# A fused adaLN, linear-attention and SwiGLU kernel: the load order of row tile 2 and the division of the first row tiles' normalisation and values

## The chip, the cores and the metric

The kernel runs on one core of one Trainium2 chip. The metric is the device time of one execution in microseconds (us); before the change its median over three runs is 828.99 us (828.73 to 829.15). Five engines work beside each other on the core, each in its own order: TensorE (PE in the profile; its weight loads are PEld), VectorE (DVE), ScalarE (ACT), GpSimd (POOL) and SyncE (SP), which here only issues transfers. Transfers (DMA) fetch from the chip's memory into on-chip tiles; matmuls write into PSUM tiles.

## The reference, cut to what matters

```python
def reference(A_x, A_wqkv, A_wo, B_x, B_w_gate, B_w_up, B_w_down, c, w_mod):
    # _A_ref: linear attention, 32 heads; q, k, v = h @ wqkv; phi(q) (sum phi(k) v) / (phi(q) sum phi(k)), @ wo
    # _B_ref: (silu(x @ w_gate) * (x @ w_up)) @ w_down
    x = A_x                                              # (1, 2048, 1024), bfloat16
    mod = (_silu(c) @ w_mod).reshape(c.shape[0], 6, 1, -1)
    sa, ca, ga, sb, cb, gb = (mod[:, 0].copy(), ..., mod[:, 5].copy())
    h = _layernorm(x, axis=-1) * (1 + ca) + sa
    x = x + ga * _A_ref(h, A_wqkv, A_wo)
    h = _layernorm(x, axis=-1) * (1 + cb) + sb
    x = x + gb * _B_ref(h, B_w_gate, B_w_up, B_w_down)
    return x
```

The change is in the opening alone: the layer norm of the first four row tiles (128 rows of 1024 each), their scale `1 + ca`, and the value projection `h @ wqkv[:, 2D:]` of those 512 rows. The shift `sa` has no part in these first values (it is put in later as one row), so they need only the normalised rows, turned, and times the scale.

## The kernel before: the opening

Loads are issued in program order on SyncE's queue. A block of weights is 128 x 1024 in bfloat16, 256 KB, and so is a row tile. The first half of the scale's weights is `wca[0]` (four pieces of 256 KB, the first from ScalarE's queue), the second half `wca[1]`; `wsa` are the shift's weights.

```python
    for st in range(3):
        load_x(st, nc.sync)
    nc.scalar.dma_start(out=c_sb[:], in_=c_v)
    # ... tiles ...
    load_ca(0, nc.scalar)
    nc.scalar.dma_start(out=sc_row[0:1, :], in_=c)
    for cc in range(4):
        load_block(wv, wqkv_v, cc, 2 * D)
    load_ca(1, nc.sync)
    load_x(3, nc.sync)
    for cc in range(4, DC):
        load_block(wv, wqkv_v, cc, 2 * D)
    for j in range(DC):
        load_block(wsa, wm_v, j, 0)
    for cc in range(DC):
        load_block(wk, wqkv_v, cc, D)
```

The statistics of a row tile are two `bn_stats` and a `bn_aggr` on VectorE, a small add there, and a power on GpSimd; `normalise_act` does a further small operation on GpSimd and then the tile on ScalarE. `bn` is a generator, so that its three steps can be laid between other VectorE work.

```python
    def rstd_of(mv, n):
        veps = small.tile([P, STC], F32, name="veps")
        last_veps[0] = nc.vector.tensor_scalar_add(out=veps[:, 0:n], in0=mv[:, 0:n, 1], scalar1=LN_EPS)
        rstd = small.tile([P, STC], F32, name="rstd")
        nc.gpsimd.tensor_tensor(out=rstd[:, 0:n], in0=veps[:, 0:n], in1=neg_half[:].to_broadcast([P, n]), op=ALU.pow)
        return rstd

    def bn(src, mv_out):
        stats = small.tile([P, NNB, nc.vector.BN_STATS_DIM], F32, name="stats")
        for i in range(NNB):
            nc.vector.bn_stats(out=stats[:, i, :], in_=src[:, i * NB:(i + 1) * NB])
            yield
        nc.vector.bn_aggr(out=mv_out, in_=stats[:])
        yield

    def normalise_act(dst, src, mv, rstd, pieces=1):
        nmr = small.tile([P, 1], F32, name="nmr")
        last_nmr[0] = nc.gpsimd.tensor_scalar(out=nmr[:], in0=mv[:, 0, 0:1], scalar1=rstd[:, 0:1], scalar2=-1.0,
                                op0=ALU.mult, op1=ALU.mult)
        w = src.shape[-1] // pieces
        for i in range(pieces):
            ws = slice(i * w, (i + 1) * w)
            nc.scalar.activation(out=dst[:, ws], in_=src[:, ws], func=ACT.Identity, bias=nmr[:], scale=rstd[:, 0:1])
```

The opening proper. `in_order` keeps VectorE, ScalarE and GpSimd in this order each; matmuls and transposes keep program order too. [...] `hs` holds the turned, scaled rows, `hT` the turned ones without scale. `v_mms(hs, gs, accs, lo, hi)` issues, for each column block `cc` from lo to hi, one 128 x 512 matmul for each group (row tile, half of the values) in `gs`.

```python
    H = 2 * P
    with in_order(nc.vector, nc.scalar, nc.gpsimd):
        mod_ps = acc_b("mod_ps")
        mm(mod_ps[:, 0:DC], lhsT=c_sb[:], rhs=ident[0:DC, 0:DC], start=True, stop=True)
        nc.scalar.activation(out=scT[:], in_=mod_ps[:, 0:DC], func=ACT.Silu)
        xn0 = ln1_norm(*ln1_stats(0, 0), 2)
        _, _, x1_sb, mv1, rstd1 = ln1_stats(0, 1)
        x2_sb = x_tiles.pop(2)
        mv2 = small.tile([P, STC, 2], F32, name="mv")
        bn2 = bn(x2_sb, mv2[:, 0, :])
        next(bn2)
        xn1 = k2.tile([P, D], BF16, name="xn", bufs=4)
        nc.vector.tensor_scalar(out=xn1[:, 0:NB], in0=x1_sb[:, 0:NB], scalar1=mv1[:, 0, 0:1], scalar2=rstd1[:, 0:1],
                                op0=ALU.subtract, op1=ALU.mult)
        normalise_act(xn1[:, NB:], x1_sb[:, NB:], mv1, rstd1)
        next(bn2)
        col0 = acc_b("col0")
        cols = [col0[:, 0:1]] + [mod_ps[:, DC + i:DC + i + 1] for i in range(3)]
        tps = [acc_b("tp", (4, H), BF16) for _ in range(2)]

        def turn_half(xn, t, h):
            for i in range(4):
                transpose(tps[h][:, i, t * P:(t + 1) * P], xn[:, (4 * h + i) * P:(4 * h + i + 1) * P])

        def ca_cols(k):
            for i in range(4):
                for j in (2 * k, 2 * k + 1):
                    mm(cols[i], lhsT=wca[0][:, j, i * P:(i + 1) * P], rhs=scT[:, j:j + 1], start=False,
                       stop=j == DC - 1 and i in (0, 3))

        mm(cols[0], lhsT=ident[:], rhs=base_t[:, 0:1], start=True, stop=False)
        keep_warm(P)
        mm(mod_ps[:, DC:DC + 3], lhsT=ident[:], rhs=base_t[:, 0:3], start=True, stop=False)
        keep_warm(2 * P)
        ca_cols(0)
        keep_warm(2 * P, P)
        ca_cols(1)
        turn_half(xn0, 0, 0)
        ca_cols(2)
        keep_warm(P)
        turn_half(xn0, 0, 1)
        turn_half(xn1, 1, 0)
        ca_cols(3)
        keep_warm(P)

        def scale_first(cc):
            nc.vector.tensor_scalar(out=hs[:, cc, 0:H], in0=tps[0][:, cc, :], scalar1=cols[cc], scalar2=None, op0=ALU.mult)

        scale_first(0)
        next(bn2)
        rstd2 = rstd_of(mv2, 1)
        for cc in range(1, 4):
            scale_first(cc)
        nc.scalar.copy(out=ca0T[:, 0:1], in_=cols[0])
        nc.scalar.copy(out=ca0T[:, 1:4], in_=mod_ps[:, DC:DC + 3])
        xn2 = ln1_norm(0, 2, x2_sb, mv2, rstd2)
        nc.scalar.copy(out=hT[:, 0:4, 0:H], in_=tps[0][:])
        nc.vector.tensor_copy(out=sc32[:], in_=scT[:].unsqueeze(2).to_broadcast([P, DC, DH]))
        gs = k_groups[0:4]
        v_mms(hs, gs, accs, 0, 1)
        turn_half(xn1, 1, 1)
        nc.scalar.copy(out=hT[:, 4:8, 0:H], in_=tps[1][:])
        nc.scalar.activation(out=sc_row[0:1, :], in_=sc_row[0:1, :], func=ACT.Silu)
        v_mms(hs, gs, accs, 1, 3)
        tp2 = turn_tile(xn2)
        for cc in range(4):
            scale_turned(tp2, cc, 2)
        nc.scalar.copy(out=hT[:, :, H:H + P], in_=tp2[:])
        v_mms(hs, gs, accs, 3, 4)
        ca_rows()
        mod_turn(DC + 4, 2 * DC)
        nc.vector.tensor_scalar_add(out=ca0T[:, 4:8], in0=ca0T[:, 4:8], scalar1=1.0)
        for cc in range(4, DC):
            scale_to(hs, hT, cc, 0, H)
        gs2, accs2 = k_groups[4:6], [acc_b("acc") for _ in range(2)]
        v_mms(hs, gs2, accs2, 0, 4)
        xn3 = ln1_norm(*ln1_stats(0, 3))
        for cc in range(4, DC):
            scale_to(hs, hT, cc, H, H + P)
        v_mms(hs, gs, accs, 4, DC)
        v_evac(0, gs, accs)
        v_mms(hs, gs2[0:1], accs2[0:1], 4, DC)
        tp3 = turn_tile(xn3)
        for cc in range(DC):
            scale_turned(tp3, cc, 3)
        nc.scalar.copy(out=hT[:, :, H + P:], in_=tp3[:])
        v_mms(hs, gs2[1:2], accs2[1:2], 4, DC)
        v_evac(0, gs2, accs2)
        gs3, accs3 = k_groups[6:8], [acc_a() for _ in range(2)]
        v_mms(hs, gs3[0:1], accs3[0:1])
        mod_rows(lambda j: wsa[j // 4][:, j % 4, :], 0, DC)
        mod_turn(0, DC)
        nc.vector.tensor_copy(out=sca[:], in_=scr[:, :, :, 0])
        v_mms(hs, gs3[1:2], accs3[1:2])
        v_evac(0, gs3, accs3)
        for lo in (0, H):
            for cc in range(DC):
                modulate(hT, cc, ca1T, saT, lo, lo + H)
        nc.vector.tensor_copy(out=sc32[:], in_=saT.unsqueeze(2).to_broadcast([P, DC, DH]))
```

Here `scale_first(cc)` is one VectorE operation `hs[:, cc, 0:256] = tps[0][:, cc, :] * cols[cc]`, which reads PSUM; `keep_warm` are matmuls whose result is overwritten; `ca_rows` are 32 narrow matmuls for the second half of the scale, `mod_rows` 32 for the shift and the rest; `mod_turn` turns their rows into columns on VectorE. After this part the keys (`k_mms`) follow, which read `hT` as `modulate` left it, and then the rest of the kernel, the same before and after.

Of the kernel before, what the change touches and what calls it, by code (L numbers as in the profile page):

```python
# [21 lines left out]
def kernel(  # L22
# [100 lines left out]
        last_load[0] = eng.dma_start(out=x_sb[:], in_=x2[st * P:(st + 1) * P, :])  # L123
        x_tiles[st] = x_sb

    for st in range(3):
        load_x(st, nc.sync)
    nc.scalar.dma_start(out=c_sb[:], in_=c_v)

# [5 lines left out]
    def load_block(tiles, view, cc, lo, eng=nc.sync):  # L135
        eng.dma_start(out=tiles[cc // 4][:, cc % 4, :], in_=view[:, cc, lo:lo + D])

    def load_ca(h, eng0):
        for k in range(4):
            js = slice(2 * k, 2 * k + 2)  # L140
            (eng0 if k == 0 else nc.sync).dma_start(out=wca[h][:, js, :], in_=wm_v[:, js, D + h * NB:D + (h + 1) * NB])
# [2 lines left out]
    nc.scalar.dma_start(out=sc_row[0:1, :], in_=c)  # L144
    for cc in range(4):
        load_block(wv, wqkv_v, cc, 2 * D)
    load_ca(1, nc.sync)
    load_x(3, nc.sync)
    for cc in range(4, DC):
# [55 lines left out]
    def bn(src, mv_out):  # L205
        stats = small.tile([P, NNB, nc.vector.BN_STATS_DIM], F32, name="stats")
        for i in range(NNB):
            nc.vector.bn_stats(out=stats[:, i, :], in_=src[:, i * NB:(i + 1) * NB])
            yield
        nc.vector.bn_aggr(out=mv_out, in_=stats[:])  # L210
        yield

    def normalise_act(dst, src, mv, rstd, pieces=1):
        nmr = small.tile([P, 1], F32, name="nmr")
# [11 lines left out]
    def turn_tile(xn):  # L226
# [2 lines left out]
            transpose(tp[:, cc, :], xn[:, cc * P:(cc + 1) * P])  # L229
        return tp  # L230

    hTs = {}

    def ln1_stats(sc, t):
        x_sb = x_tiles.pop(sc * STC + t)
        mv = small.tile([P, STC, 2], F32, name="mv")
        for _ in bn(x_sb, mv[:, 0, :]):
            pass
        rstd = rstd_of(mv, 1)
        return sc, t, x_sb, mv, rstd  # L240

# [224 lines left out]
    def keep_warm(*widths):  # L466
        for n in widths:
            mm(accs[3][:, 0:n], lhsT=neg_half[:].to_broadcast([P, P]), rhs=neg_half[:].to_broadcast([P, n]), start=True, stop=True)
# [8 lines left out]
# [3 lines that stand above are left out]
        nc.scalar.activation(out=scT[:], in_=mod_ps[:, 0:DC], func=ACT.Silu)  # L480
        xn0 = ln1_norm(*ln1_stats(0, 0), 2)
        _, _, x1_sb, mv1, rstd1 = ln1_stats(0, 1)
        x2_sb = x_tiles.pop(2)
        mv2 = small.tile([P, STC, 2], F32, name="mv")
        bn2 = bn(x2_sb, mv2[:, 0, :])
        next(bn2)
        xn1 = k2.tile([P, D], BF16, name="xn", bufs=4)
        nc.vector.tensor_scalar(out=xn1[:, 0:NB], in0=x1_sb[:, 0:NB], scalar1=mv1[:, 0, 0:1], scalar2=rstd1[:, 0:1],
                                op0=ALU.subtract, op1=ALU.mult)
        normalise_act(xn1[:, NB:], x1_sb[:, NB:], mv1, rstd1)  # L490
        next(bn2)
        col0 = acc_b("col0")
        cols = [col0[:, 0:1]] + [mod_ps[:, DC + i:DC + i + 1] for i in range(3)]
        tps = [acc_b("tp", (4, H), BF16) for _ in range(2)]
# [17 lines that stand above are left out]
        ca_cols(1)  # L512
        turn_half(xn0, 0, 0)
        ca_cols(2)
        keep_warm(P)
        turn_half(xn0, 0, 1)
        turn_half(xn1, 1, 0)
        ca_cols(3)
        keep_warm(P)

        def scale_first(cc):
            nc.vector.tensor_scalar(out=hs[:, cc, 0:H], in0=tps[0][:, cc, :], scalar1=cols[cc], scalar2=None, op0=ALU.mult)

        scale_first(0)
        next(bn2)
        rstd2 = rstd_of(mv2, 1)
        for cc in range(1, 4):
            scale_first(cc)
        nc.scalar.copy(out=ca0T[:, 0:1], in_=cols[0])
        nc.scalar.copy(out=ca0T[:, 1:4], in_=mod_ps[:, DC:DC + 3])  # L530
        xn2 = ln1_norm(0, 2, x2_sb, mv2, rstd2)
        nc.scalar.copy(out=hT[:, 0:4, 0:H], in_=tps[0][:])
        nc.vector.tensor_copy(out=sc32[:], in_=scT[:].unsqueeze(2).to_broadcast([P, DC, DH]))
        gs = k_groups[0:4]
        v_mms(hs, gs, accs, 0, 1)
        turn_half(xn1, 1, 1)
        nc.scalar.copy(out=hT[:, 4:8, 0:H], in_=tps[1][:])
        nc.scalar.activation(out=sc_row[0:1, :], in_=sc_row[0:1, :], func=ACT.Silu)
        v_mms(hs, gs, accs, 1, 3)
        tp2 = turn_tile(xn2)  # L540
        for cc in range(4):
            scale_turned(tp2, cc, 2)
        nc.scalar.copy(out=hT[:, :, H:H + P], in_=tp2[:])
        v_mms(hs, gs, accs, 3, 4)
        ca_rows()
        mod_turn(DC + 4, 2 * DC)
        nc.vector.tensor_scalar_add(out=ca0T[:, 4:8], in0=ca0T[:, 4:8], scalar1=1.0)
        for cc in range(4, DC):
            scale_to(hs, hT, cc, 0, H)
        gs2, accs2 = k_groups[4:6], [acc_b("acc") for _ in range(2)]  # L550
        v_mms(hs, gs2, accs2, 0, 4)
        xn3 = ln1_norm(*ln1_stats(0, 3))
        for cc in range(4, DC):
            scale_to(hs, hT, cc, H, H + P)
# [8 lines that stand above are left out]
        v_evac(0, gs2, accs2)  # L563
        gs3, accs3 = k_groups[6:8], [acc_a() for _ in range(2)]
        v_mms(hs, gs3[0:1], accs3[0:1])
        mod_rows(lambda j: wsa[j // 4][:, j % 4, :], 0, DC)
        mod_turn(0, DC)
        nc.vector.tensor_copy(out=sca[:], in_=scr[:, :, :, 0])
        v_mms(hs, gs3[1:2], accs3[1:2])
        v_evac(0, gs3, accs3)  # L570
        for lo in (0, H):
            for cc in range(DC):
                modulate(hT, cc, ca1T, saT, lo, lo + H)
        nc.vector.tensor_copy(out=sc32[:], in_=saT.unsqueeze(2).to_broadcast([P, DC, DH]))
    for st in range(STC, 2 * STC):
        load_x(st, nc.sync)
# [267 lines left out]
```

## Time and profile before

| what | value | where from |
|---|---|---|
| median time | 828.99 us (828.73 to 829.15) | three runs |
| span of the profiled execution | 827.1 us | the page's head |
| PE busy | 822.5 us (99%) | the page, part 1 |
| VectorE, ScalarE, GpSimd busy | 345.9, 173.6, 65.2 us | the page, part 1 |
| first value matmul | at 9.22 us | PE's timeline |
| first key matmul | at 26.14 us | PE's timeline |
| TensorE clock granted | full in all slices | the page, part 2 |

How to read it: PE is busy for nearly all of the span, so what the opening takes on PE before and between its matmuls is passed on to the end. Times in a timeline are start and length in us. An operation's listed length is longer than its share when operations of one engine follow each other closely; the distance from one start to the next is then what each costs. Matmul ends are modelled.

### The profile page before, as it was taken

The numbers are of one execution on the slowest core, as the hardware profiler recorded it, in microseconds if no ns is written. First come the engines' busy times: TensorE is split into PE (matmuls) and PEld (weight loads), VectorE is DVE, ScalarE is ACT, GpSimd is POOL, SyncE is SP. The second block draws the span as 40 slices with busy tenths as digits, with TensorE's granted clock in tenths as the row PEclk, the third lists the DMA queues.
The fourth block names the chain that finished last, engine by engine and source line by source line (L and its number), as shares of the span: only waits on it lengthen the run. The fifth ranks groups of instructions, "written<-read, shape, count | busy, mean of one in ns | idle before, by whom it ended". The sixth has DMA issues, their size and how long they took to land.

```text
span 827.1 us, 11346 instructions
## 1 busy us (share of the span) xinstructions
PE 822.5 (99%) x4629; PEld 379.8 (46%) x4629; DVE 345.9 (42%) x683; ACT 173.6 (21%) x261; POOL 65.2 (8%) x167
## 2 busy tenths in 40 slices
PE   9999999999999999999999999999999999999998
PEld 5444444444444444444444444444444444444444
DVE  5878778886353344421111353211114432222222
ACT  5545443434111101101111010111111101111000
POOL 3101110120313001000000010000001100000000
PEclk9999999999999999999999999999999999999999
DMA  9989544149995726456252272753405529710011
GB/s 342 307 180 205 115 107 100 44 117 318 374 230 184 262 100 190 142 170 214 82 171 84 66 223 86 253 185 113 142 1 183 147 67 342 235 44 1 18 59 52
DMA packets 143414, 129.33 MB, mean 156 GB/s; under 512 B 58817, under 2 KB 122817, under 8 KB 142850
## 3 DMA queue, kind: packets, MB, share of 16 engines
q1 hardware_dynamic: 139248, 115.36, 46.6%
q0 software_dynamic: 3824, 12.98, 5.1%
q8 instruction: 36, 0.59, 0.3%
q10 hardware_dynamic: 290, 0.27, 0.1%
q14 instruction: 16, 0.13, 0.1%
HBM read 102.24 MB, written 12.72 MB: 139 GB/s over the span
## 4 chain that ended last, share of the span: by engine, by line
PE 99%; DMA 1%; SPq 0%; DVE 0%; issue 0%
PE acc L98 91%; PE a_ps L98 7%; DMA wme<-in_w_mod_dram 1%; PE kvp L98 1%; PE mod_ps L98 0%; PE tp L101 0%; PE den L98 0%; SPq L123 0%; PE wf L98 0%; PE vb L98 0%; PE col L98 0%; DVE e L760 0%; DVE ob L763 0%
## 5 line engine op out<-in xcount | busy, mean ns | idle before, releaser
L98 PE MATMUL acc<-h2T,wgu 128*128 128x512 bf16 x1792 | 387.6, 379 | 0.0
L98 PEld LDWEIGHTS <-wgu 128*128 128x128 bf16 x1792 | 175.3, 98 | 211.3
L739 DVE TENSOR_TENSOR gu<-acc,e 128x512 bf16<-128x512 f32 x112 | 77.4, 691 | 289.9 <-PE acc L98 287.1
L98 PE MATMUL acc<-wd,gu 128*128 128x512 bf16 (+2 forms) x924 | 196.1, 373 | 0.0
L738 ACT ACTIVATE e<-acc 128x512 f32<-128x512 f32 x112 | 66.9, 597 | 374.8 <-PE acc L98 374.8
L98 PEld LDWEIGHTS <-gu 128*128 128x128 bf16 x924 | 89.3, 98 | 104.5
L760 DVE TENSOR_TENSOR e<-acc,gb_bc 128x512 f32<-128x512 f32 (+2 forms) x33 | 22.3, 675 | 131.6 <-PE acc L98 128.7
L98 PEld LDWEIGHTS <-hT 128*128 128x128 bf16 x448 | 43.6, 98 | 52.3
L98 PE MATMUL a_ps<-wof,pq 128*128 128x512 bf16 x256 | 57.4, 379 | 0.0
L98 PE MATMUL acc<-hT,wq 128*128 128x512 bf16 x256 | 56.6, 379 | 0.0
L98 PE MATMUL acc<-wk,hT 128*128 128x512 bf16 x256 | 56.4, 379 | 0.0
L284 ACT ACTIVATE eb<-acc 128x512 bf16<-128x512 f32 x64 | 37.5, 594 | 60.3 <-PE acc L98 56.6
L220 ACT ACTIVATE xn<-x,nmr,rstd 128x1024 bf16<-128x1024 f32 x16 | 19.8, 1241 | 126.2 <-POOL nmr L215 123.2
L98 PE MATMUL acc<-wv,hT 128*128 128x512 bf16 x192 | 41.9, 379 | 0.0
L707 POOL DMA_DIRECT2D x_scratch<-x x16 | 9.8, 615 | 373.5 <-DVE x L700 373.4
L98 PEld LDWEIGHTS <-pq 128*128 128x128 bf16 x256 | 25.1, 98 | 30.2
L98 PEld LDWEIGHTS <-wq 128*128 128x128 bf16 x256 | 24.7, 98 | 30.7 <-issue 1.7
L285 DVE TENSOR_SCALAR eb<-eb 128x512 bf16<-128x512 bf16 x64 | 18.2, 289 | 26.4 <-ACT eb L284 26.4
L700 DVE TENSOR_TENSOR x<-a_ps,x_sb 128x512 f32<-128x512 f32 x32 | 22.1, 691 | 8.6 <-PE a_ps L98 8.6
L202 POOL TENSOR_TENSOR rstd<-veps,neg_half 128x1 f32<-128x1 f32 x32 | 18.0, 562 | 91.8 <-DVE veps L200 70.1
L220 ACT ACTIVATE xn<-x_sb,nmr,rstd 128x1024 bf16<-128x1024 bf16 (+1 forms) x17 | 19.5, 1163 | 16.0 <-POOL nmr L215 15.9
L763 DVE TENSOR_TENSOR ob<-e,x1r 128x512 bf16<-128x512 f32 (+2 forms) x33 | 22.3, 675 | 1.0
(106 smaller groups left out, 330.0 us busy)
## 6 DMA issues: line engine op xcount, KB each, us to landing
wgu<-in_B_w_gate_dram SPq DMA_DIRECT2D x28, 1024.0 KB, 7.3
wgu<-in_B_w_up_dram SPq DMA_DIRECT2D x28, 1024.0 KB, 8.1
x_sb<-in_A_x_dram SPq DMA_DIRECT2D x32, 256.0 KB, 5.3
x_scratch<-x POOLq DMA_DIRECT2D x16, 512.0 KB, 3.3
x1r<-x_scratch SPq DMA_DIRECT2D x31, 256.0 KB, 2.9
wd<-in_B_w_down_dram SPq DMA_DIRECT2D x7, 1024.0 KB, 5.8
rbc<-rden_scratch POOLq DMA_DIRECT2D x16, 256.0 KB, 7.1
out_dram<-ob SPq DMA_DIRECT2D x31, 128.0 KB, 1.7
```

Of the source, the lines that this page charges most:

```text
L98: return tc.keep_in_program_order(nc.tensor.matmul(out, lhsT=lhsT, rhs=rhs, start=start, stop=stop))
L202: nc.gpsimd.tensor_tensor(out=rstd[:, 0:n], in0=veps[:, 0:n], in1=neg_half[:].to_broadcast([P, n]), op=ALU.pow)
L220: nc.scalar.activation(out=dst[:, ws], in_=src[:, ws], func=ACT.Identity, bias=nmr[:], scale=rstd[:, 0:1])
L284: nc.scalar.activation(out=e[:], in_=acc, func=ACT.Exp)
L285: nc.vector.tensor_scalar(out=e[:], in0=e[:], scalar1=1.0, scalar2=PHI_EPS, op0=ALU.min, op1=ALU.add)
L700: nc.vector.tensor_tensor(out=x1[:, ns], in0=a_ps[:], in1=x_t[:, ns], op=ALU.add)
L707: nc.gpsimd.dma_start(out=x1_dram[st * P:(st + 1) * P, :], in_=x1[:])
L738: nc.scalar.activation(out=sg[:], in_=ps[0][:], func=ACT.Silu)
L739: gm = nc.vector.tensor_tensor(out=guT[sc][f // GPT][:, f % GPT, :], in0=ps[1][:], in1=sg[:], op=ALU.mult)
L760: nc.vector.tensor_tensor(out=yt, in0=y_ps, in1=gb_bc[:, ns], op=ALU.mult)
L763: nc.vector.tensor_tensor(out=ob, in0=yt, in1=x1r, op=ALU.add)
```

## The change

It delays the load of row tile 2 until the first value-weight block is issued, so that the pieces of `wca[0]` and that block come one place earlier on the queue. Row tile 1 is normalised on VectorE in one operation instead of half there and half on ScalarE. Tile 2's statistics move behind the scaling of the first rows, and its normalisation is divided between VectorE and ScalarE. Both halves of tile 1 are turned before the first value matmul. Tile 2's transposes are divided into four before and four after the second scale rows (`ca_rows`), with the first value matmuls of tile 2 around those. Two `keep_warm` go. At the end of the part, the last values lie partly before `mod_rows`, and the eight `modulate` of `hT` take 512 columns each where sixteen took 256.

```diff
--- before.py
+++ after.py
@@ -123,7 +123,7 @@
         last_load[0] = eng.dma_start(out=x_sb[:], in_=x2[st * P:(st + 1) * P, :])
         x_tiles[st] = x_sb
 
-    for st in range(3):
+    for st in range(2):
         load_x(st, nc.sync)
     nc.scalar.dma_start(out=c_sb[:], in_=c_v)
 
@@ -144,6 +144,8 @@
     nc.scalar.dma_start(out=sc_row[0:1, :], in_=c)
     for cc in range(4):
         load_block(wv, wqkv_v, cc, 2 * D)
+        if cc == 0:
+            load_x(2, nc.sync)
     load_ca(1, nc.sync)
     load_x(3, nc.sync)
     for cc in range(4, DC):
@@ -206,9 +208,7 @@
         stats = small.tile([P, NNB, nc.vector.BN_STATS_DIM], F32, name="stats")
         for i in range(NNB):
             nc.vector.bn_stats(out=stats[:, i, :], in_=src[:, i * NB:(i + 1) * NB])
-            yield
         nc.vector.bn_aggr(out=mv_out, in_=stats[:])
-        yield
 
     def normalise_act(dst, src, mv, rstd, pieces=1):
         nmr = small.tile([P, 1], F32, name="nmr")
@@ -229,13 +229,19 @@
             transpose(tp[:, cc, :], xn[:, cc * P:(cc + 1) * P])
         return tp
 
+    def norm_split(src, mv, rstd):
+        xn = k2.tile([P, D], BF16, name="xn", bufs=4)
+        nc.vector.tensor_scalar(out=xn[:, 0:NB], in0=src[:, 0:NB], scalar1=mv[:, 0, 0:1], scalar2=rstd[:, 0:1],
+                                op0=ALU.subtract, op1=ALU.mult)
+        normalise_act(xn[:, NB:], src[:, NB:], mv, rstd)
+        return xn
+
     hTs = {}
 
     def ln1_stats(sc, t):
         x_sb = x_tiles.pop(sc * STC + t)
         mv = small.tile([P, STC, 2], F32, name="mv")
-        for _ in bn(x_sb, mv[:, 0, :]):
-            pass
+        bn(x_sb, mv[:, 0, :])
         rstd = rstd_of(mv, 1)
         return sc, t, x_sb, mv, rstd
 
@@ -480,15 +486,9 @@
         nc.scalar.activation(out=scT[:], in_=mod_ps[:, 0:DC], func=ACT.Silu)
         xn0 = ln1_norm(*ln1_stats(0, 0), 2)
         _, _, x1_sb, mv1, rstd1 = ln1_stats(0, 1)
-        x2_sb = x_tiles.pop(2)
-        mv2 = small.tile([P, STC, 2], F32, name="mv")
-        bn2 = bn(x2_sb, mv2[:, 0, :])
-        next(bn2)
         xn1 = k2.tile([P, D], BF16, name="xn", bufs=4)
-        nc.vector.tensor_scalar(out=xn1[:, 0:NB], in0=x1_sb[:, 0:NB], scalar1=mv1[:, 0, 0:1], scalar2=rstd1[:, 0:1],
+        nc.vector.tensor_scalar(out=xn1[:], in0=x1_sb[:], scalar1=mv1[:, 0, 0:1], scalar2=rstd1[:, 0:1],
                                 op0=ALU.subtract, op1=ALU.mult)
-        normalise_act(xn1[:, NB:], x1_sb[:, NB:], mv1, rstd1)
-        next(bn2)
         col0 = acc_b("col0")
         cols = [col0[:, 0:1]] + [mod_ps[:, DC + i:DC + i + 1] for i in range(3)]
         tps = [acc_b("tp", (4, H), BF16) for _ in range(2)]
@@ -512,43 +512,45 @@
         ca_cols(1)
         turn_half(xn0, 0, 0)
         ca_cols(2)
-        keep_warm(P)
         turn_half(xn0, 0, 1)
+        ca_cols(3)
         turn_half(xn1, 1, 0)
-        ca_cols(3)
-        keep_warm(P)
-
-        def scale_first(cc):
-            nc.vector.tensor_scalar(out=hs[:, cc, 0:H], in0=tps[0][:, cc, :], scalar1=cols[cc], scalar2=None, op0=ALU.mult)
-
-        scale_first(0)
-        next(bn2)
-        rstd2 = rstd_of(mv2, 1)
+        turn_half(xn1, 1, 1)
+
+        def scale_first(cc, lo, hi):
+            nc.vector.tensor_scalar(out=hs[:, cc, lo:hi], in0=tps[0][:, cc, lo:hi], scalar1=cols[cc], scalar2=None, op0=ALU.mult)
+
+        scale_first(0, 0, P)
+        scale_first(0, P, H)
         for cc in range(1, 4):
-            scale_first(cc)
+            scale_first(cc, 0, H)
         nc.scalar.copy(out=ca0T[:, 0:1], in_=cols[0])
         nc.scalar.copy(out=ca0T[:, 1:4], in_=mod_ps[:, DC:DC + 3])
-        xn2 = ln1_norm(0, 2, x2_sb, mv2, rstd2)
         nc.scalar.copy(out=hT[:, 0:4, 0:H], in_=tps[0][:])
-        nc.vector.tensor_copy(out=sc32[:], in_=scT[:].unsqueeze(2).to_broadcast([P, DC, DH]))
         gs = k_groups[0:4]
         v_mms(hs, gs, accs, 0, 1)
-        turn_half(xn1, 1, 1)
         nc.scalar.copy(out=hT[:, 4:8, 0:H], in_=tps[1][:])
-        nc.scalar.activation(out=sc_row[0:1, :], in_=sc_row[0:1, :], func=ACT.Silu)
-        v_mms(hs, gs, accs, 1, 3)
-        tp2 = turn_tile(xn2)
+        _, _, x2_sb, mv2, rstd2 = ln1_stats(0, 2)
+        nc.vector.tensor_copy(out=sc32[:], in_=scT[:].unsqueeze(2).to_broadcast([P, DC, DH]))
+        xn2 = norm_split(x2_sb, mv2, rstd2)
+        v_mms(hs, gs, accs, 1, 4)
+        tp2 = acc_b("tp", (DC, P), BF16)
+        for cc in range(4):
+            transpose(tp2[:, cc, :], xn2[:, cc * P:(cc + 1) * P])
         for cc in range(4):
             scale_turned(tp2, cc, 2)
-        nc.scalar.copy(out=hT[:, :, H:H + P], in_=tp2[:])
-        v_mms(hs, gs, accs, 3, 4)
+        gs2, accs2 = k_groups[4:6], [acc_b("acc") for _ in range(2)]
+        v_mms(hs, gs2, accs2, 0, 2)
         ca_rows()
         mod_turn(DC + 4, 2 * DC)
         nc.vector.tensor_scalar_add(out=ca0T[:, 4:8], in0=ca0T[:, 4:8], scalar1=1.0)
         for cc in range(4, DC):
             scale_to(hs, hT, cc, 0, H)
-        gs2, accs2 = k_groups[4:6], [acc_b("acc") for _ in range(2)]
-        v_mms(hs, gs2, accs2, 0, 4)
+        for cc in range(4, DC):
+            transpose(tp2[:, cc, :], xn2[:, cc * P:(cc + 1) * P])
+        nc.scalar.copy(out=hT[:, :, H:H + P], in_=tp2[:])
+        nc.scalar.activation(out=sc_row[0:1, :], in_=sc_row[0:1, :], func=ACT.Silu)
+        v_mms(hs, gs2, accs2, 2, 4)
         xn3 = ln1_norm(*ln1_stats(0, 3))
         for cc in range(4, DC):
             scale_to(hs, hT, cc, H, H + P)
@@ -563,14 +565,13 @@
         v_evac(0, gs2, accs2)
         gs3, accs3 = k_groups[6:8], [acc_a() for _ in range(2)]
         v_mms(hs, gs3[0:1], accs3[0:1])
+        v_mms(hs, gs3[1:2], accs3[1:2], 0, 2)
         mod_rows(lambda j: wsa[j // 4][:, j % 4, :], 0, DC)
         mod_turn(0, DC)
         nc.vector.tensor_copy(out=sca[:], in_=scr[:, :, :, 0])
-        v_mms(hs, gs3[1:2], accs3[1:2])
+        v_mms(hs, gs3[1:2], accs3[1:2], 2, DC)
         v_evac(0, gs3, accs3)
-        for lo in (0, H):
-            for cc in range(DC):
-                modulate(hT, cc, ca1T, saT, lo, lo + H)
+        modulate_all(hT, ca1T, saT)
         nc.vector.tensor_copy(out=sc32[:], in_=saT.unsqueeze(2).to_broadcast([P, DC, DH]))
     for st in range(STC, 2 * STC):
         load_x(st, nc.sync)
```

## The prediction

> **What bounds the kernel now.** The page's chain of the work that ended last comes first: PE takes 99% of it, so only what TensorE does, or waits for, can move the end. The waits of PE come next, over the whole span:
>
> ```profile
> PE 99%; DMA 1%; SPq 0%; DVE 0%; issue 0%
> PE acc L98 <- DVE neg_half L159: 0.9, 1, 0.9
> PE col L98 <- DMA wme<-in_w_mod_dram: 0.6, 1, 0.6
> ```
>
> PE waits 1.5 us in all, and all of it lies before the first value matmul. Behind that point nothing later can swallow a shift: a microsecond lost or won in the opening is a microsecond at the end. So I read PE's timeline of the opening (start, length, operation, count):
>
> ```profile
> 7.27 0.40 PE L101 MATMUL tp<-ident,xn 128*128 128x128 bf16 x4
> 9.22 1.04 PE L98 MATMUL acc<-wv,hs 128*128 128x512 bf16 x4
> 10.10 0.39 PE L101 MATMUL tp<-ident,xn 128*128 128x128 bf16 x4
> 10.32 1.89 PE L98 MATMUL acc<-wv,hs 128*128 128x512 bf16 x8
> 12.05 0.61 PE L101 MATMUL tp<-ident,xn 128*128 128x128 bf16 x8
> 12.49 1.03 PE L98 MATMUL acc<-wv,hs 128*128 128x512 bf16 x4
> 13.45 0.84 PE L98 MATMUL mod_ps<-wme,sc 128*32 128x128 bf16 x32
> 14.23 6.22 PE L98 MATMUL acc<-wv,hs 128*128 128x512 bf16 x28
> ```
>
> From 9.22 to the first key matmul at 26.14 there is no hole: 28 matmuls from 14.23 to 20.28 are 0.216 us each, eight transposes from 12.05 to 12.49 are 0.055 each, `ca_rows` from 13.45 to 14.23 is 0.78. What feeds this is VectorE's timeline:
>
> ```profile
> 6.89 0.68 DVE L208 BATCH_NORM_STATS2 stats<-x_sb 128x6 f32<-128x512 bf16 x1
> 7.65 0.41 DVE L488 TENSOR_SCALAR xn<-x_sb,mv,rstd 128x512 bf16<-128x512 bf16 x1
> 7.97 0.69 DVE L208 BATCH_NORM_STATS2 stats<-x_sb 128x6 f32<-128x512 bf16 x1
> 8.81 0.35 DVE L522 TENSOR_SCALAR hs<-tp,col 128x256 bf16<-128x256 bf16 x1 [0.15 <-PE col L98]
> 9.08 0.20 DVE L210 BATCH_NORM_AGGREGATE mv<-stats 128x2 f32<-128x12 f32 x1
> 9.40 0.88 DVE L522 TENSOR_SCALAR hs<-tp,mod_ps 128x256 bf16<-128x256 bf16 x3
> 12.77 0.86 DVE L277 TENSOR_SCALAR hs<-tp,e 128x128 bf16<-128x128 bf16 x4 [2.29 <-PE tp L101]
> ```
>
> Two things are to be seen. Tile 2's statistics (6.89 and 7.97) sit in holes in which VectorE waits for GpSimd or PE, so they cost nothing. And the scaling of tile 2 at 12.77 waits for all eight transposes (modelled end 12.05 + 0.61 = 12.66), though its first operation reads only one; meanwhile PE has matmuls and `ca_rows` up to 14.23.
>
> [...] `modulate` takes 0.34 us for 256 columns and 0.41 for 512, so 0.07 per 256 more, and the PSUM reads 0.274 for 128 and 0.35 for 256, so 0.07 per 128. [...] the record gives the full clock throughout, with a hole of 0.6 us.
>
> **Part 1, the load.** `wca[0]`'s last three pieces and the first `wv` block move up by 256 KB. From 5 to 10 us the queues move 383 GB/s, so 0.262 MB / 383 GB/s = 0.7 us earlier. This removes the wait of 0.6 at 6.33 to 6.94, but the next thing on PE is the transposing of tile 0, which starts at 7.27 because ScalarE's first half of it, from 6.40, takes 0.8. Tiles 0 and 1 land first in either version, and VectorE goes from 3.63 to 6.97 with hardly a hole. So the earlier weights alone win nothing: they end in a longer wait for tile 0. Tile 2 becomes the eighth block, 2.1 MB: 1.0 MB by 5 us (203 GB/s x 5), the other 1.1 at 383 GB/s, so at 7.9, plus about 1 us until it is seen (that offset is from the fifth block: 1.31 MB have passed at 5.8 by the same sum, and PE was let go at 6.9). At 8.9 it is in time for what follows.
>
> **Part 2, the first value matmul.** The power for tile 1 still ends at 7.61, so VectorE's whole-tile normalisation starts at 7.65. Its 1024 columns take 0.41 + 2 x 0.07 = 0.55: to 8.20. On PE, tile 0's second half (ready at 7.92, 6.40 + 1.52) is turned from 7.98 to 8.20, eight scale columns take 0.21 (8.56 to 8.77 before) to 8.41, four transposes of tile 1 go to 8.63, four more to 8.85. [...] `scale_first(0, 0, P)` waits for the first four: 8.41 + 0.39 = 8.80. It runs from 8.85 to 9.12, and the first value matmul starts 0.06 later (that is 8.06 to 8.12 for tile 1 before), at **9.18**. Before it was 9.22, but with four transposes (0.22) still to come. Won: 0.04 + 0.22 = **0.26 us**. The second `scale_first` piece is done at 9.33, before the third matmul needs it at 9.61.
>
> **Part 3, tile 2.** After those two pieces (0.2 apart) come three scalings, 0.26 apart: 9.25, 9.51, 9.77; the statistics follow at 10.03. From a tile's first `bn_stats` to the normalisation on VectorE it was 5.26 to 7.65 for tile 1, 2.39 us, bound by the statistics, the aggregate, the small add and GpSimd's power. The same from 10.03 gives 12.42, and the half tile (0.41) ends at 12.83; transposes can start at 12.89. PE has 16 matmuls from 9.18: 16 x 0.216 = 3.46, to 12.64. **It waits 0.25.** Then four transposes, modelled end 12.89 + 0.39 = 13.28; VectorE starts about 0.08 later (0.04 and 0.11 seen before), takes 0.27, and PE starts tile 2's values 0.06 after: 13.69. Without the wait for VectorE they would have started at 12.89 + 0.22 = 13.11. **It waits 0.58**, as the program has no other PE work between the four transposes and the matmuls that need their scaled result. In the kernel before, four matmuls and `ca_rows` lay there.
>
> Then four matmuls with 0.1 for the change to narrow tiles (13.45 - 12.49 = 0.96 for four before), to 14.65; `ca_rows` to 15.43; four transposes to 15.65; four matmuls to 16.52; 16 to 19.98; four to 20.84. ScalarE's half of tile 2, normalised by about 13.7, is there for the later transposes.
>
> **Part 4, tile 3.** Before, it was normalised at 18.56 + 1.24 = 19.80, which is 5.57 after `ca_rows` left PE at 14.23, through the row turn, four scalings, the statistics, GpSimd and ScalarE; the chain is the same now. From 15.43 that is 21.00, so transposes at 21.06, but PE is there at 20.84, because fewer matmuls lie behind `ca_rows` (24 and four transposes, against 28). **It waits 0.22.**
>
> **Part 5, the end of the part.** Behind `mod_rows` six matmuls are left where there were eight: 1.30 us. Before, `mod_rows` left PE at 24.40 and the first `modulate` started at 25.22; with 0.41 for 512 columns it ends 1.23 after, and 0.06 more makes 1.29. **No wait, or a few hundredths.** The following `modulate` are about 0.33 apart, and a pair of key matmuls takes 0.43, so they keep ahead. Eight operations fewer on VectorE save it 8 x 0.26 less 8 x 0.07, some 1.5 us, off the path.
>
> **The sum:** -0.26 + 0.25 + 0.58 + 0.22 = **+0.79 us**. I chose +0.7 for the forecast, because every handover above has been counted in full and the DVE-to-PE ones may overlap with weight loads. 828.99 + 0.7 = **829.7 us**.
>
> **Rivals.** (a) *The earlier start carries through.* If tile 2's chain were faster than I count, by 0.25, and the handover of 0.58 partly hidden, the change would be near zero, 828.9; if tile 0 and tile 1 also landed earlier with one transfer less in front of them, it would be 828.5. For it speaks that the only DMA wait of PE is one of the loads moved; against it, that tiles 0 and 1 are ahead of tile 2 in both versions, and that the transposes of tile 0 follow that wait by only 0.33. (b) *The transfers become the wait.* `wv` blocks 1 to 3 are wanted earlier (10.05, 10.91, 11.78 against 10.32, 11.18 and 12.66) while their places in the queue stay: blocks 9 to 11, seen at about 9.6, 10.2 and 10.9. They just fit; a wait there would partly stand in place of the 0.25, so the time would be 829.7 to 830.2. (c) *The clock.* Without two `keep_warm`, PE has about 1.4 us of holes between 6.3 and 9.2. [...] The record before, at full clock with fewer holes, neither shows nor excludes it; I give it one in fifteen.
>
> **Range and chances.** The sum's terms are each uncertain by 0.1 to 0.3, together some 0.5, and (a) reaches further down than (b) goes up: 828.6 to 830.5. The whole opening before the keys is 26 us, 3% of the time, and no rival comes near 2% (16.6 us): within 2% 0.98, and 0.01 for each side.
>
> **What would show it.** In the changed kernel's PE timeline: the first value matmul at 9.1 to 9.2 with eight transposes of tile 1 ahead of it; a hole near 12.6 that VectorE's `xn` ends, and one of half a microsecond that VectorE's `hs` ends; `ca_rows` starting near 14.7; a small hole at tile 3's transposes; the first key matmul near 26.9. PE's list of waits should gain about 1 us on VectorE and ScalarE, and the wait for `wme` should turn into one for `xn`. Wrong would be: a first key matmul before 26.14, a value matmul at 8.9 or earlier [...], or a clock below full.

## The result, and the profile after

The changed kernel takes 831.73 us in the median of six runs (830.19 to 832.54), the kernel before 829.10 (828.73 to 829.95): a ratio of 1.0029, with a 95% interval of 1.0016 to 1.0042. It is slower by some 2.6 us. The forecast was 829.7 with a range of 828.6 to 830.5, so the direction was right and the size was not.

The record of the changed kernel has a span of 829.9 us against 827.1. PE's waits (what waited, for whom: us in total, times, longest):

```profile
PE acc L98 <- DVE neg_half L161: 0.9, 1, 0.9
PE acc L98 <- issue: 0.8, 2, 0.5
PE acc L98 <- ACT xn L220: 0.5, 1, 0.5
```

The wait for `wme` (the profile's name for the pieces of `wca`) is gone, as meant. In its place stands a wait in tile 2's first values, put down to ScalarE's half of `xn`, which came last by the record; what these matmuls read is VectorE's scaled `hs`. New is the middle line, "issue": 0.8 us in which PE waited for nothing that the profile shows. PE's timeline of the opening:

```profile
4.36 0.78 PE L98 MATMUL acc<-neg_half 128*128 128x128 f32 x2
5.00 1.20 PE L98 MATMUL acc<-neg_half 128*128 128x256 f32 x2
9.21 1.01 PE L101 MATMUL tp<-ident,xn 128*128 128x128 bf16 x8
10.19 3.67 PE L98 MATMUL acc<-wv,hs 128*128 128x512 bf16 x16
13.87 0.40 PE L101 MATMUL tp<-ident,xn 128*128 128x128 bf16 x4
14.73 1.04 PE L98 MATMUL acc<-wv,hs 128*128 128x512 bf16 x4 [0.46 <-ACT xn L220]
15.70 0.63 PE L98 MATMUL mod_ps<-wme,sc 128*32 128x128 bf16 x32
21.99 0.62 PE L101 MATMUL tp<-ident,xn 128*128 128x128 bf16 x8
27.91 13.99 PE L98 MATMUL acc<-wk,hT 128*128 128x512 bf16 x64
```

Three things are to be seen. Eight transposes take 1.01 where before they took 0.61: up to about 10 us TensorE works at half rate in this execution (these transposes start 0.107 apart, before 0.056), and the first value matmul comes at 10.19 instead of the 9.18 forecast. From there to the first key matmul it is 17.72 us; the forecast had 17.7. But the first key matmul is 1.77 later than before (26.14), and the span 2.8 longer: 1.03 us are lost behind it, in code that the change does not touch. The timeline there, around the first and third block of 128 `kvp` matmuls (keys times values, 64 columns each):

```profile
57.36 1.22 PE L98 MATMUL kvp<-v,pk 128*32 128x64 bf16 x128
58.52 0.82 PE L98 MATMUL acc<-wk,hT 128*128 128x512 bf16 x3
59.87 2.32 PE L98 MATMUL acc<-wk,hT 128*128 128x512 bf16 x10 [0.53 <-issue]
...
116.98 0.61 PE L98 MATMUL acc<-wk,hT 128*128 128x512 bf16 x2
117.89 2.32 PE L98 MATMUL acc<-wk,hT 128*128 128x512 bf16 x10 [0.30 <-issue]
```

PE stops in the middle of a group of eight matmuls, after the third and after the second, with nothing to release it. Before, 56 matmuls follow either block without a hole:

```profile
56.87 12.26 PE L98 MATMUL acc<-wk,hT 128*128 128x512 bf16 x56
114.64 12.26 PE L98 MATMUL acc<-wk,hT 128*128 128x512 bf16 x56
```

### The profile page after: what moved, and what is told of

Same layout as the page of the kernel before. It is cut to its first block, busy times and chain, and to the rows that moved or that the text cites. A ratio compares the mean times of both kernels' runs of the same rounds, so it can differ in the third digit from the quotient of the medians.

```text
span 829.9 us, 11328 instructions
## 1 busy us (share of the span) xinstructions
PE 824.5 (99%) x4625; PEld 380.6 (46%) x4625; DVE 345.9 (42%) x677; ACT 172.7 (21%) x260; POOL 64.6 (8%) x166
## 4 chain that ended last, share of the span: by engine, by line
PE 98%; DVE 1%; ACT 0%; POOL 0%; issue 0%; DVEq 0%
PE acc L98 90%; PE a_ps L98 7%; PE kvp L98 1%; DVE stats L210 0%; PE mod_ps L98 0%; PE tp L101 0%; ACT xn L220 0%; PE den L98 0%; DVE hs L521 0%; POOL rstd L204 0%; PE wf L98 0%; DVE hs L279 0%; PE vb L98 0%; POOL nmr L215 0%; DVE mv L211 0%
## 5 line engine op out<-in xcount | busy, mean ns | idle before, releaser
L702 DVE BATCH_NORM_STATS2 stats<-x 128x6 f32<-128x512 f32 x32 | 22.1, 693 | 1.0
```

The costliest lines, as they stand in the source:

```text
L702: nc.vector.bn_stats(out=stats[:, nb, :], in_=x1[:, ns])
```

## The experiments

The theories after the result: A and B, the half rate is chance, or the missing `keep_warm` bring it on; C, the moved load does; D, the late holes hang on PE's own instruction stream; and the chain of tile 2, as forecast.

**The change once more, and with `keep_warm`.** First the same kernel again.

> The changed kernel once more, unaltered, for a second record of its opening. Theory A (the clock of TensorE rose late by chance of that one execution): transposes 0.055 us apart and the first value matmul near 9.2, first key matmul near 26.9, time near 830. Theory B (something in the change itself keeps TensorE at half rate to about 10 us): transposes again 0.11 us apart, first value matmul near 10.2, time near 831.7. On the two later holes of PE behind the blocks of 128 kvp matmuls (0.5 and 0.3 us): if they come from when an execution gets its instructions, they sit elsewhere or are missing here.

Median 831.30 (lowest 830.52), ratio 1.0026 (1.0019 to 1.0034). The record is an execution in which full rate came at about 6.1: first value matmul 9.05, first key matmul 26.77. So the half rate to 10 us is not always there, and without it the opening costs 26.77 - 26.14 = 0.63. The late hole was there again, 0.95 at 58.2 and none at the third block: same place, other size.

```diff
         ca_cols(2)
+        keep_warm(P)
         turn_half(xn0, 0, 1)
         ...
         turn_half(xn1, 1, 1)
+        keep_warm(P)
```

> The changed kernel with the two keep_warm put back (one ahead of the second half of tile 0, one ahead of the first value matmul). Theory B in the form that the missing keep_warm cost the clock: TensorE is at full rate before 8 us, first value matmul near 9.3, first key matmul near 27.0, time near 830.2, 1.5 below the changed kernel. Rival (the keep_warm have no part in it): half rate as before, the added matmuls only cost, time 831.7 to 832.5.

Median 829.64 (lowest 829.46), ratio 1.0008 (0.9999 to 1.0017). First key matmul at 26.83, no late hole. Its lowest time lies about 0.7 above that of the kernel before (828.79), which is what the chain of tile 2 was forecast to cost. The two `keep_warm` were worth over 1.5 us in the median, but the record does not say why: the opening of `after_again` without them was just as quick.

**The kernel before without them**

```diff
         ca_cols(2)
-        keep_warm(P)
         ...
         ca_cols(3)
-        keep_warm(P)
```

> The kernel before without the same two keep_warm. If their absence costs the clock: half rate until about 10 us, first value matmul near 10, time near 830. If not: first value matmul at 9.2 as before, time 829.0 within 0.3.

Median 830.50 (lowest 829.84), ratio 1.0013 (1.0005 to 1.0020). The removal alone costs about 1 us, in another kernel. Its record again has the late holes, 0.52 and 0.58, and again after three and after two matmuls (the first matmul behind a block is missing from that record). It also has half rate to 13.8 us.

**The load alone**

```diff
-    for st in range(3):
+    for st in range(2):
         load_x(st, nc.sync)
     ...
         load_block(wv, wqkv_v, cc, 2 * D)
+        if cc == 0:
+            load_x(2, nc.sync)
```

> The kernel before with only the load of tile 2 moved behind the first value-weight block. By the prediction the earlier weights win nothing, because PE waits next for tile 0: first value matmul at 9.2, unless the statistics of tile 2, which this kernel still takes before tile 1 is normalised, now hold VectorE until tile 2 has landed (about 8.9): then tile 1 is normalised near 9.7 instead of 8.1, and the time is 1.5 above, near 830.6. Theory C (the moved load itself disturbs the clock of TensorE): half rate to about 10 us.

Median 830.55, ratio 1.0018 (1.0011 to 1.0025). VectorE stood in tile 2's statistics until its data came, and PE with it:

```profile
10.09 0.40 PE L101 MATMUL tp<-ident,xn 128*128 128x128 bf16 x4 [1.71 <-DVE xn L490]
```

So the later load needs the later statistics; the two parts belong together. The record starts at full rate, so theory C falls. After the hole it lost that: eight value matmuls from 12.61 took 3.04 where 1.89 is normal, and the trace's clock record has half rate from 11.51 to 14.92. Seven other runs resemble it: eight of the 20 lie at 831.86 to 832.54, with a mean granted clock of 0.998 or 0.999, and twelve at 830.11 to 830.80 with 1.000.

**The chain of tile 2 and the load, in the changed kernel with `keep_warm`.** First the matmuls of the fourth column block moved behind tile 2's first transposes, to fill the handover:

```diff
-        v_mms(hs, gs, accs, 1, 4)
+        v_mms(hs, gs, accs, 1, 3)
         ...
+        v_mms(hs, gs, accs, 3, 4)
         v_mms(hs, gs2, accs2, 0, 2)
```

> The changed kernel with both keep_warm, and with the four value matmuls of the fourth column block moved from ahead of tile 2's transposes to behind the first four, so that PE has 0.87 us of work while VectorE scales them. If the handover to VectorE costs about half a microsecond as predicted: the hole after the four transposes is gone, but the wait for tile 2's normalisation ahead of them grows by up to 0.87; together PE waits for tile 2's chain alone, so 0.5 less than the same kernel without the move at most (829.0 against 829.5), and nothing at all if that chain (statistics to transposes) is what ends last.

Median 829.71, lowest 829.57, ratio 1.0009 (1.0002 to 1.0016): 0.1 more than without the move.

```profile
12.81 0.40 PE L101 MATMUL tp<-ident,xn 128*128 128x128 bf16 x4 [0.92 <-DVE xn L234]
13.04 1.89 PE L98 MATMUL acc<-wv,hs 128*128 128x512 bf16 x8
```

The handover is filled (matmuls follow the transposes at once), and the whole of it comes back ahead of the transposes, which can't start before VectorE's half of tile 2 at about 12.75. The statistics of tile 2 are what ends last.

> The changed kernel with both keep_warm and with the load of tile 2 back in third place. If the moved load wins nothing, as predicted, the first value matmul stays at 9.1 and the time at 829.5 within 0.2. If it does win: a wait of PE for wme of about 0.6 comes back and the first value matmul and the end are later by 0.3 or more.

Here `load_x(2)` stands third again. Median 829.62, lowest 829.48, ratio 1.0007 (0.9998 to 1.0015): the same as with the load moved. In the record, an execution of 829.85, PE does wait for `wme` (0.7 in two waits) and the first value matmul is at 9.49, so in some executions the moved load wins 0.4 (9.49 against 9.11); it does not show in median or lowest.

**Tile 1 in one piece, in the kernel before**

```diff
-        nc.vector.tensor_scalar(out=xn1[:, 0:NB], ...); normalise_act(xn1[:, NB:], ...)
+        nc.vector.tensor_scalar(out=xn1[:], ...)
         ...
         turn_half(xn0, 0, 1)
-        turn_half(xn1, 1, 0)
         ca_cols(3)
-        keep_warm(P)
+        turn_half(xn1, 1, 0); turn_half(xn1, 1, 1)
+        keep_warm(P)
         ...
         v_mms(hs, gs, accs, 0, 1)
-        turn_half(xn1, 1, 1)
```

> The kernel before with one part of the change: tile 1 normalised on VectorE in one piece, the last scale columns ahead of its transposes, and both its halves turned ahead of the first value matmul. By the prediction's part 2 the first value matmul stays near 9.25 with four transposes fewer behind it: 0.2 us won, 828.8 (lowest 828.6). If the whole-tile operation delays the first scaling instead: first value matmul near 9.4 and no gain.

Median 829.16 (lowest 828.73), ratio 0.9997 (0.9989 to 1.0006). The 0.2 us do not show. Its record can't tell about its opening at full rate, because it is another execution with half rate to about 10 us, though both `keep_warm` are there; it shows that these do not prevent that.

**The length of PE's stream.** Does theory D hold? One tiny matmul was put at 5 us, where PE has time:

```diff
         keep_warm(2 * P)
+        mm(accs[3][:, 0:1], lhsT=ident[:], rhs=base_t[:, 0:1], start=True, stop=True)
         ca_cols(0)
```

> The changed kernel with one tiny matmul (its weight load and itself, two instructions) put ahead of the first scale columns, where PE has time to spare; the two keep_warm stay away. In the records so far PE has two holes without a releaser of 0.3 to 1.0 us, always at the same instructions (three matmuls after the first block of 128 kvp matmuls, two after the third), in every kernel that has 9226 PE instructions and in none that has 9228. Theory D (the holes hang on where in PE's instruction stream these matmuls lie, so PE waits for its own instructions): with 9228 again the holes are gone, the lowest times fall from 830.5 to about 829.6. Rival (the holes hang on the work of keep_warm, its clock or power): holes stay, lowest times 830.5.

Median 830.93 (lowest 829.75), ratio 1.0018 (1.0010 to 1.0027). The holes stayed, so the theory in this form fell; but they had moved:

```profile
56.45 1.22 PE L98 MATMUL kvp<-v,pk 128*32 128x64 bf16 x128
57.83 0.38 PE L98 MATMUL acc<-wk,hT 128*128 128x512 bf16 x1 [0.16 <-issue]
58.51 3.83 PE L98 MATMUL acc<-wk,hT 128*128 128x512 bf16 x17 [0.31 <-issue]
```

A hole of 0.16 straight behind a block is the place of a matmul missing from the record; the same 0.16 stands in records without any loss (here 4548 recorded matmuls stand for 4626 weight loads). So the real hole, 0.31, now comes after two matmuls and no longer after three: one matmul with its weight load, that is two instructions, earlier. Behind the third block PE went on at 116.85, after a gap of 0.95 with one missing matmul in it. My count had been wrong, not the idea. By the page's first part the kernel before has 4629 weight loads and the changed one 4625: each `keep_warm` of this width stands as two loads and two matmuls (before, from 8.77: `acc<-neg_half` 128x128 f32 x2), so the change took eight instructions away and the tiny matmul gave back two.

With `for _ in range(4)` ahead of that line, eight are given back, and with `range(2)` four:

> The changed kernel with four tiny matmuls ahead of the first scale columns. In the records each keep_warm stands as two weight loads and two matmuls, so the change took eight instructions from PE's stream and one tiny matmul gave two back; with it the two holes came two instructions earlier in the program. Four give back all eight. Theory D (the holes hang on how far into the stream the blocks of kvp matmuls lie): no hole without a releaser from 27 us on beyond 0.16, lowest times near 829.5, as with the two keep_warm. Rival (keep_warm itself is needed): holes as before, lowest times 829.8 to 830.5.

Median 829.45 (lowest 829.42), ratio 1.0000 (0.9991 to 1.0009). No hole is left:

```profile
56.27 1.22 PE L98 MATMUL kvp<-v,pk 128*32 128x64 bf16 x128
57.66 4.70 PE L98 MATMUL acc<-wk,hT 128*128 128x512 bf16 x21 [0.16 <-issue]
...
115.43 4.91 PE L98 MATMUL acc<-wk,hT 128*128 128x512 bf16 x22 [0.16 <-issue]
```

Four one-column matmuls added make the changed kernel nearly 2 us faster in the median, without `keep_warm`.

> The changed kernel with two tiny matmuls at the same place: four of the eight instructions given back. Theory D: a hole one matmul earlier again (one matmul after the first block of kvp matmuls), or none; lowest times between 829.5 and 830.1. Rival: as the changed kernel, lowest 830.2 to 830.5.

Median 830.41 (lowest 829.57), ratio 1.0015 (1.0009 to 1.0022): in its record gaps of 0.57 and 0.56 close behind the two blocks.

> The kernel before without the two keep_warm (which was 0.9 to 1.3 above the kernel before) but with four tiny matmuls in the early opening. Theory D: no holes after 27 us, and the time is that of the kernel before, lowest near 828.8, median 829.0 to 829.4. Rival (the clock needs the two keep_warm): lowest 829.8, median 830.5 as without the tiny matmuls.

Median 829.10 (lowest 828.95), ratio 1.0000 (0.9992 to 1.0009), against 830.50 without the four: the rival, that the clock needs the two `keep_warm`, falls in this kernel too.

> The kernel before with only the last part of the change: two of the last value matmuls ahead of mod_rows, and modulate in eight operations of 512 columns. By the prediction's part 5: no wait of PE ahead of the first key matmul beyond 0.05, lowest time 828.8 as before. Rival: a wait of 0.2 to 0.4 there, 829.1.

This is `v_mms(hs, gs3[1:2], accs3[1:2], 0, 2)` ahead of `mod_rows` and `modulate_all` in the kernel before. Lowest 829.04, median 829.53, ratio 1.0002 (0.9993 to 1.0011). From the first value to the first key matmul 26.07 - 9.07 = 17.00 against 16.92, and the wait ahead of the first key matmul is 26.07 - (23.72 + 0.99 + 6 x 0.216) = 0.06. So the record fits the forecast, but the lowest time is nearer to the rival's 829.1 than to 828.8. A cost of 0.1 to 0.3 is possible and not shown.

**The half rate.** The four tiny matmuls once more, now at 25 us, behind the opening:

```diff
+        for _ in range(4):
+            mm(mod_ps[:, 0:1], lhsT=ident[:], rhs=base_t[:, 0:1], start=True, stop=True)
         mod_rows(lambda j: wsa[j // 4][:, j % 4, :], 0, DC)
```

> The changed kernel with the four tiny matmuls placed at 24 us, ahead of mod_rows, instead of at 5 us. Up to there TensorE does what it does in the changed kernel; behind it the instruction stream is eight longer, as in the kernel before. Theory D: no holes behind the kvp matmuls; lowest times 829.5 to 829.7 (up to 0.2 for the four, now on the path). For the half rate of TensorE up to 10 us: if the change (its opening without keep_warm) brings it on, about half of the executions still lie 1 us or more above the lowest and the median is near 830.7; if it comes by chance in any of these kernels, and the tiny matmuls at 5 us had no part in that, the times lie as with those: median within 0.2 of the lowest, few above.

Median 829.89 (829.42 to 830.66 in 13 runs), ratio 1.0005 (0.9997 to 1.0014). Again no holes, so it doesn't matter whether the instructions stand at 5 or at 25 us. Six runs lie at 829.42 to 829.54, three at 829.89 to 830.09, four at 830.62 to 830.66; the record is one of these four, with the first value matmul at 10.18 instead of 9.06 and no other difference of size. So half rate up to 10 us costs 1.1 to 1.2. The kernel before, run beside it, has five of 17 at 830.0 and above. About a third in both. Taken together, 5 of the 25 runs of `after_pad8` and this kernel lie 1.1 us or more above their lowest, 13 of the 44 of the three versions with `keep_warm`, and 46 of the 173 of the kernel before at 829.9 and above: neither the opening of the change nor the missing `keep_warm` visibly brings it on once the stream has its old length.

The loss behind the opening, as span less the start of the first recorded key matmul:

| kernel | weight loads of PE | first key | span | difference |
|---|---|---|---|---|
| before | 4629 | 26.14 | 827.1 | 800.96 |
| after | 4625 | 27.91 | 829.9 | 801.99 |
| after_again | 4625 | 26.77 | 828.7 | 801.93 |
| before_nokeep | 4625 | 28.57 | 831.0 | 802.43 |
| after_pad2 | 4626 | 26.79 | 829.1 | 802.31 |
| after_pad4 | 4627 | 26.80 | 828.5 | 801.70 |
| after_keep | 4629 | 26.83 | 827.7 | 800.87 |
| after_pad8 | 4629 | 26.77 | 827.7 | 800.93 |
| after_pad8_late | 4629 | 27.97 | 828.8 | 800.83 |
| before_nokeep_pad8 | 4629 | 26.21 | 827.3 | 801.09 |

With 4629 it is 800.8 to 801.1 whichever opening stands ahead (the five records not listed, all with 4629, give 800.9 to 801.1); with fewer it is 0.7 to 1.5 more.

## Why the prediction was wrong, point by point

**Part 1, the load: right.** "The earlier weights alone win nothing" holds in median and lowest time of the pair with and without it, and PE's wait for `wme` became one for tile 0.

**Parts 2 to 5, at full rate: the sum nearly right, two terms not.** The opening of `after_pad8`, on PE:

```profile
9.06 3.67 PE L98 MATMUL acc<-wv,hs 128*128 128x512 bf16 x15 [0.16 <-DVE hs L523]
12.74 0.40 PE L101 MATMUL tp<-ident,xn 128*128 128x128 bf16 x4
13.59 1.04 PE L98 MATMUL acc<-wv,hs 128*128 128x512 bf16 x4 [0.46 <-ACT xn L220]
14.56 0.63 PE L98 MATMUL mod_ps<-wme,sc 128*32 128x128 bf16 x32
15.12 0.40 PE L101 MATMUL tp<-ident,xn 128*128 128x128 bf16 x4
...
20.85 0.62 PE L101 MATMUL tp<-ident,xn 128*128 128x128 bf16 x8
```

| term | forecast | measured | how |
|---|---|---|---|
| first value matmul, and four transposes done | -0.26 | -0.38 | 9.06 - 9.22 - 0.22 |
| tile 2's normalisation | +0.25 | +0.22 | 12.74 - (9.06 + 16 x 0.216) |
| handover to VectorE | +0.58 | +0.63 | 13.59 - (12.74 + 0.22) |
| `ca_rows` | 0 | -0.22 | (15.12 - 14.56) - (14.23 - 13.45) |
| tile 3 | +0.22 | +0.32 | 20.85 - (15.12 + 0.23 + 24 x 0.216) |
| first key | 0 to 0.05 | +0.06 | 26.77 - (24.42 + 0.99 for `mod_rows` + 6 x 0.216) |
| sum | +0.79 | +0.63 | first key 26.77 - 26.14 = 0.63 |

That the sums are so near is in part luck: the errors in `ca_rows` (-0.22) and tile 3 (+0.10) have opposite signs.

In the third row the profile names ScalarE's `xn`; what the matmuls read is `hs`, which VectorE wrote after its half. `xn` of tile 1 took 0.55 on VectorE, as forecast, and the first scaling started behind the first four of tile 1's eight transposes, as forecast: at 9.84 in the changed kernel's record (modelled end of the four 9.21 + 0.59 = 9.80, at half rate), at 8.71 in `after_pad8` (8.29 + 0.40 = 8.69). In both the profile names PE's `tp` as what ended VectorE's wait (1.79 and 0.64); why VectorE waits for these four, it does not show.

The forecast took 0.78 for `ca_rows` from the kernel before, and missed a wait inside it. In the records where it starts at 13.2 to 13.5 its 32 matmuls take 0.74 to 0.81, in all where it starts at 14.5 or later 0.56 to 0.57. So this one move of the change does win 0.2; that the early ones wait for the last piece of `wca[1]` fits, but no record names it. For tile 3 the forecast missed GpSimd's queue. Its timeline in `after_pad8`:

```profile
17.82 0.74 POOL L584 DMA_DIRECT2D sc_scratch<-sc_row  x1 [5.09 <-ACT sc_row L554]
18.60 0.56 POOL L204 TENSOR_TENSOR rstd<-veps,neg_half 128x1 f32<-128x1 f32 x1
```

The power for tile 3 could start about 0.1 after the small add (before, 17.57 after 17.47), here by 18.47, but stands behind the issue of a transfer until 18.60, because ScalarE's `Silu` of `sc_row` now comes later; before, that issue was over at 15.7.

**The step that failed** is the first: "Behind that point nothing later can swallow a shift: a microsecond lost or won in the opening is a microsecond at the end." Shifts did pass on. But the step took the rest of the span to be fixed, and it isn't: what the opening leaves out of PE's instruction stream moves every later instruction in it. Two `keep_warm` fewer made late holes, of 0.8 to 1.1 us together without the 0.16 of missing matmuls, in every record without the full count, and giving the eight instructions back, at 5 us or at 25 us, closed them: the median fell from 831.30 to 829.45 in the changed kernel, and from 830.50 to 829.10 in the kernel before without `keep_warm`. The prediction weighed the two `keep_warm` for the clock alone.

**The rivals.** (c), the clock: half rate is in the record of the changed kernel, and it cost 1.1 of the 2.8 us between the two records. But full rate came late there (at 10.31) rather than fell; this is seen with the `keep_warm` too (`before_piece`), and without them it is no more frequent once the stream has its length (one of 12 in `after_pad8`, four of 13 in `after_pad8_late`). A fall stands in one record only, `before_load`, for 3.41 (11.51 to 14.92) and behind a hole of 1.71; the two groups of its runs lie about 1.7 apart, which is what 3.41 at half rate lose (half of it, an estimate from that record). That the hole brought the fall on, one record does not show. Rival (a) fell, since the handover measured 0.63 and was not hidden. Rival (b) did not occur in the changed kernel.

**The sum of the medians.** 0.63 of the opening and about 1.0 of holes make 1.6 of the 2.6 us; the lowest times differ by 830.19 - 828.73 = 1.46. The 0.63 is a difference of records at full rate. For `after_pad8` and the kernel before run beside it the lowest times differ by 829.42 - 828.69 = 0.73, but the medians by only 0.27, which is not clear of noise. The rest fits executions with late full rate: 12 of the changed kernel's 21 runs lie above 831.7. But the holes differ from run to run as well, so its times alone don't tell the two apart, and whether it has more late executions than the kernel before stays open.

No version beat both: `before_nokeep_pad8`, `before_piece` and the kernel before can't be told apart.

## What to carry to other kernels

Taking instructions out can cost time far from where they stood: here four to eight fewer, ahead of 9 us, cost 0.7 to 1.5 us behind the first key matmul. When the timeline shows a hole with no releaser, as here always some matmuls behind a dense block of short ones, count PE's instructions in both kernels, look when the packets of the instruction queue come (here each hole ended 1.3 to 1.6 us after one), and pad the shorter kernel before explaining the hole by the change itself. No stream longer than the old one was tried here. And take several records before reading one: here a single record mixed a cost of the change (0.6), one of the stream's length (1.0) and one of chance (1.1).

## What was not expected of the hardware

**PE's stream.** The page's list of queues has this line (packets, MB, share):

```profile
q8 instruction: 36, 0.59, 0.3%
```

In the trace each of the 36 packets has 16,384 bytes, and from one to the next PE runs 252 of its recorded weight loads and matmuls on average (8832 in 35 intervals, 152 to 363 in one, in the kernel before). The line does not say whose instructions they carry. A `kvp` block has 128 + 128 = 256 loads and matmuls, so about one packet's worth by that average, which is an estimate. The block runs them in 1.15 us, where ordinary matmuls take 128 x 0.216 = 28 us for as many. The trace also has the time of each packet. Here it is for the nine holes, in us from the start of the block ahead of the hole:

| record, block | packet ended | PE went on | difference |
|---|---|---|---|
| after, first | 1.09 | 2.51 | 1.42 |
| after, third | 0.73 | 2.06 | 1.33 |
| after_again, first | 1.37 | 2.93 | 1.56 |
| before_nokeep, first | 1.10 | 2.49 | 1.39 |
| before_nokeep, third | 0.80 | 2.34 | 1.54 |
| after_pad2, first | 0.74 | 2.06 | 1.32 |
| after_pad2, third | 0.85 | 2.17 | 1.32 |
| after_pad4, first | 0.22 | 1.80 | 1.58 |
| after_pad4, third | 0.17 | 1.79 | 1.62 |

In all nine, PE goes on 1.3 to 1.6 us after a packet has ended. Among the first three blocks of these five records six have no hole, and there the packet ended at 0.20 at the latest (0.17 left a hole in `after_pad4`, but there the hole lies at most one matmul behind the block, so PE came to it earlier). In the ten records with the full count it ended 0.31 or more ahead of the block's start, at each of the 30 blocks. So in every one of these 45 blocks the times fit a wait for a late packet of instructions; that the packet is what releases PE the trace does not name. How so few instructions bring it forward stays open: ahead of the third block the packet starts 4.2 to 4.7 us before the block with the full count and 0.1 to 0.8 with fewer, while four ordinary matmuls are only 4 x 0.216 = 0.86.

**Half rate and the profile.** The granted clock in the page stands at full in all slices of all records, and the forecast took it so ("full clock throughout"). But the trace's clock record has nothing ahead of its first entry, and the page counts that stretch as full (1.00 from 0.9 to 10.3 in the changed kernel). The first entry, at full rate, begins at 4.25 us in the record before and at 10.31 in the changed kernel's, and there the distance between matmuls halves (transposes 0.107 apart up to 9.91, 0.056 from 21.99). Over all 15 records it begins at 3.9 to 6.2 in eleven, at 9.8 to 10.5 in three and at 13.8 in `before_nokeep`. The durations in the trace have one step in common: full rate lasted 819.20, 822.61 or 826.03 us in 14 records, which is 240, 241 and 242 times 3.413, and the half rate inside `before_load` lasted 3.413. Less whole steps of 3.413, the first entry leaves 0.5 to 2.8 us in all eleven early records (one step) and 2.9 to 3.6 in the four late ones (two or three). So chance, here where the steps lie when an execution begins, fits all 15; this is an estimate of mine from those times, and what decides the rate of a step no run here shows.
